# A transformer kernel on one core: maxima bank by bank, and its loads cut into pieces and put in another order

## The chip, the cores and the metric

The kernel runs on 1 core of one Trainium2 chip. The metric is the device time of one execution in microseconds. Before the change three runs took 503.15, 505.49 and 505.87 us: the median is 505.49 us.

## The reference

Batch 2, 12 heads, 448 tokens, head size 64. First an attention that mixes its heads before and after the softmax, then two blocks of multi-layer mixing. q, k, v are 32 bit; the weights of the two later blocks come as 64-bit floats and are turned into 32-bit pairs (high and low) on the chip.

```python
scores = scale * np.matmul(q, k.transpose(0, 1, 3, 2))
scores = np.einsum('bhij,hg->bgij', scores, w_pre)
scores = scores - np.max(scores, axis=-1, keepdims=True)
attn = np.exp(scores)
attn = attn / (np.sum(attn, axis=-1, keepdims=True) + 1e-09)
attn = np.einsum('bhij,hg->bgij', attn, w_post)
attn_out = np.matmul(attn, v)
...
u = x + (np.maximum(x.T @ w_tok1, 0) @ w_tok2).T
x = u + np.maximum(u @ w_ch1, 0) @ w_ch2
h = gelu(x @ w_in); u, v = halves(h); v_n = layer norm of v
out = x + (u * (w_sg @ v_n + b_sg)) @ w_out
```

## The kernel before, in words

**Chunks.** The rows of each batch are cut into four chunks (`CH`, line 45: 120, 120, 120 and 88 rows). For one chunk and one pair of heads `qk` (line 318) multiplies q by k: eight matmuls into a PSUM tile of two banks, which ScalarE or VectorE then copies into the score tile S of the chunk. Chunks 0 and 1 are computed ahead of the loop (lines 520 to 525); `COPIES` (line 518) says which engine copies which pair of heads, and for the last pair of each of these two chunks the copy is split: one engine takes the first bank, the other the second. Later chunks' `qk` are spread over the steps (lines 526 to 531).

**Steps.** A step works on 20 rows of a chunk with all 12 heads (the last step of a batch on 8 rows). There are 46 steps, 23 for each batch. For a step, `b_dma` (line 352) moves scores from S into two P tiles by DMA (210 KB each), heads and rows now on the partitions. `b_pre` mixes heads by matmuls into a PSUM pair, two banks for two groups of rows; `b_max` (line 369) takes the negative maximum of each row, both banks by one VectorE reduction; `b_exp` is one ScalarE instruction per bank with the maximum as bias and the sum as second output; `b_norm` on GpSimd inverts the sums and scales the mixing weights; `b_post` (line 399) mixes heads again with 64 small matmuls; `b_turn` copies the result into AT. Once a chunk is complete, `av` (line 425) multiplies AT by v and copies the two banks of its PSUM pair, the first by ScalarE, the second by VectorE (line 457).

**Order.** The order on each engine is written out by hand in the loop of line 566, which runs from -5 to 45. In turn i stand `b_pre`, `b_max` and `b_exp` of step i + 2 (`LP`), `b_norm` of step i + 1, `b_post` and `b_turn` of step i, an `av` where one is due, then on SP's queue `b_dma` of step i + 5 (`LD`), and after it the loads that the list at line 537 gives for that turn. There are eight P tiles, so the `b_dma` of step i + 5 waits until the pre of step i + 1 has read its tiles. `b_dma` of step 0 stands ahead of the loop (line 565), its second half on ScalarE's queue; all other loads but one are on SP's queue.

**Loads.** `load_q` brings half of the q of a chunk (192 KB), `load_v` a third of v (448 KB), `load_k` one pair of heads of k or two (`KG`, line 309: 224 KB, once 448 KB). The first four weight pieces (448 to 512 KB, "early", line 82) are loaded in attention, one at a time: the first from the list at turn 6, each following one when the piece ahead of it has been converted.

**The pump.** `conv_steps` (line 160) is a generator that converts the weight pieces: absolute value on ScalarE, a clamp (for early pieces on GpSimd), three bit operations on VectorE, a cast on ScalarE, a subtraction on GpSimd, about one instruction for each turn of the generator. In attention the loop turns it once a step from step 8 on (`pump(1)`, line 596). An early piece takes eight turns in all, the fourth one seven.

Of the kernel before, what the change touches and what calls it, by code (L numbers as in the profile page):

```python
# [8 lines left out]
F32 = mybir.dt.float32  # L9
F32R = mybir.dt.float32r  # L10
U32 = mybir.dt.uint32
# [4 lines left out]
ALU = mybir.AluOpType  # L16
AX = mybir.AxisListType
PSUM = bass.MemoryType.PSUM

LD, LP = 5, 2  # L20
NP_BUFS = 2 * (LD - LP + 1)
# [9 lines left out]
def tile_kernel(ctx, tc, q, k, v, w_pre, w_post, w_tok1, w_tok2, w_ch1, w_ch2,  # L31
                w_u, w_v, g_ln, w_sg, b_sg, w_out, out):
    nc = tc.nc
    B, D, H, S = 2, 64, 12, 448
    P = 128
    NP = H // 2
# [43 lines left out]
    wstate = {"dma": 0, "conv": 0, "room": 0, "used": 0, "bar": 0, "raw": {}, "abs": {}, "open": False}  # L80

    def early(i):

        return i <= p_t2[-1]

    def w_dma():
        i = wstate["dma"]
        if i >= len(pieces) or not (early(i) or wstate["open"]):
            return
        wstate["dma"] += 1  # L90
        src, pr, a, n = pieces[i][:4]
        wide = 1 if src.dtype == F32 else 2
        if early(i):
            raw = ap_.tile([P, 2 * EC], U32, tag="eraw", name=f"raw{i}")
        else:
            raw = wpool.tile([P, 2 * WC], U32, tag="raw", name=f"raw{i}", bufs=RB)
        r = raw[:pr, :wide * a * n].rearrange("p (a n) -> p a n", a=a)
        nc.sync.dma_start(out=r, in_=src.bitcast(U32))
        wstate["raw"][i] = r

# [59 lines left out]
    def conv_steps():  # L160
        for i in range(len(pieces)):
            while i not in wstate["raw"]:
                yield
            for _ in w_conv(i):
                yield
            wstate["conv"] = i + 1
            w_dma()
            yield
            if early(i + 1):
                yield  # L170

    def pump(n):

# [112 lines left out]
    ap_ = actx.enter_context(tc.tile_pool(name="attn", bufs=1))  # L286
    psM = actx.enter_context(tc.tile_pool(name="psM", bufs=2, space=PSUM))
    psB = actx.enter_context(tc.tile_pool(name="psB", bufs=2, space=PSUM))
# [9 lines left out]
    QG = 3  # L298
    NQ = NP // QG

    def load_v(b, g):
        t = vn[b, g] = ap_.tile([P, 14 * D], F32, tag=f"vn{g}", name=f"vn{b}_{g}")
        nc.sync.dma_start(out=t, in_=v[b, :, g])

    def load_q(b, c, g, eng=nc.sync):
        t = qn[b, c, g] = qp.tile([P, QG, P], F32, tag=f"qn{g}", name=f"qn{b}_{c}_{g}", bufs=2)
        eng.dma_start(out=t, in_=q[b, :, c, g * QG:(g + 1) * QG])

    KG = [(0, 1), (1, 1), (2, 2), (4, 1), (5, 1)]

    def load_k(b, g):
        i, n = KG[g]
# [30 lines left out]
    NB = len(steps)  # L343
# [5 lines left out]

    ring = [ap_.tile([P, S], F32, name=f"P{n}") for n in range(NP_BUFS)]  # L350

    def b_dma(i, engines=(nc.sync, nc.sync)):

        b, c, p, ne = steps[i]
        nb = CH[c][1] // (2 * IB)
        for r in range(2):
            j = 64 * r + p
            src = SS[b, c][j:j + (IB - 1) * nb + 1:nb] if ne == 2 else SS[b, c][64 * r + IB * nb:64 * r + IB * nb + HB]
            engines[r].dma_start(out=ring[(2 * i + r) % NP_BUFS][PAD:PAD + ne * HW], in_=src)

    def b_pre(i):
        ne = steps[i][3]
# [6 lines left out]
    def b_max(i):  # L369
        ne = steps[i][3]  # L370
        st[i]["nm"] = ap_.tile([P, 2], F32, tag="nm", name=f"nm{i}", bufs=3)
        nc.vector.tensor_reduce(out=st[i]["nm"][:, :ne], in_=st[i]["pre"][:, :ne, :S], axis=AX.X, op=ALU.max, negate=True)  # L372

    def b_exp(i):
        ne = steps[i][3]
# [110 lines left out]
    def add(step, fn, *a):  # L486
        extra.setdefault(step, []).append((fn, a))
# [27 lines left out]
    nc.gpsimd.memset(mone, -1.0)  # L515
    turn_over(8)

    COPIES = ((nc.scalar.copy, nc.vector.tensor_copy), (nc.vector.tensor_copy, nc.scalar.copy))
    scores = {}
    for x in range(NCH):  # L520
        if x < 2:
            at = [-LD - 1 + x] * NP
            for i in range(NP):
                n = x * NP + i
                add(at[i], qk, x, i, (psM, psB)[n % 2], COPIES[n % 2][:1 + (n == NP - 1)])
        else:
            f0, f1 = first[chunks[x - 1]] - LD, first[chunks[x]] - LD
            room = list(range(f0, f1))
            at = [room[i * len(room) // NP] for i in range(NP)]
            for i in range(NP):  # L530
                scores.setdefault(at[i], []).append((x, i))
        if x == 0:
            add(at[-1], scale_pre)
    for fn, a in extra.pop(-LD - 1):
        fn(*a)
    loads = {}
    for at, fn, *a in [(-2, load_q, 0, 2, 0), (-1, load_q, 0, 2, 1), (1, load_v, 0, 1), (3, load_v, 0, 2),
                       (4, load_q, 0, 3, 0), (6, load_q, 0, 3, 1), (6, load_q, 1, 0, 0), (6, w_dma),
                       (9, load_k, 1, 0), (9, load_k, 1, 1), (9, load_q, 1, 0, 1),
                       (12, load_k, 1, 2), (12, load_k, 1, 3), (14, load_k, 1, 4),  # L540
                       (15, load_const_late), (15, load_q, 1, 1, 0), (15, load_q, 1, 1, 1),
                       (18, load_q, 1, 2, 0), (20, load_q, 1, 2, 1), (23, load_q, 1, 3, 0), (26, load_q, 1, 3, 1),
                       (26, load_v, 1, 0), (27, load_v, 1, 1), (29, load_v, 1, 2)]:
        loads.setdefault(at, []).append((fn, a))

    X, RX = {}, {}
# [15 lines left out]
        if i + LD > NB and turns:  # L562
            turn(pair(f"xps0_{len(turns)}")[:, 0], *turns.pop(0))

    b_dma(0, (nc.sync, nc.scalar))
    for i in range(-LD, NB):
        for fn, a in extra.get(i, []):
            fn(*a)
# [18 lines left out]
            b_turn(i, nc.vector.tensor_copy if ahead else nc.scalar.copy)  # L587
            next_av(i)
        next_turn(i)
        if 0 < i + LD < NB:  # L590
            b_dma(i + LD)
        for fn, a in loads.get(i, []):
            fn(*a)
        if 0 < i + LD - NB <= RB:
            w_dma()
        if i >= 8:
            pump(1)
        if i + LD == NB:
            qctx.close()
# [412 lines left out]
```

## Time and profile before

| | |
|---|---|
| median of 3 runs | 505.49 us (503.15 to 505.87) |
| the profiled execution | 505.07 us, its span 503.3 us |
| TensorE busy | 482.0 us (96% of the span) |
| VectorE, ScalarE, GpSimd busy | 341.7, 235.5, 209.5 us |
| bytes moved | 63.84 MB, mean 127 GB/s |

Times in rows are microseconds from the start of the span. PE is TensorE, PEld its weight loads, DVE VectorE, ACT ScalarE, POOL GpSimd, SP SyncE; a q behind the name is the engine's queue of instructions that do no work of their own, such as issuing a DMA. L372 is line 372 of the kernel. A tile goes by its name without its number, as `nm<-pre`: written from read. "issue" as a releaser means that the engine waited for nothing that the profile shows. A matmul with 32-bit operands shows as two records, so four matmuls of `b_pre` are eight.

### The profile page before, as it was taken

The numbers are of one execution on the slowest core, as the hardware profiler recorded it, in microseconds if no ns is written. First come the engines' busy times: TensorE is split into PE (matmuls) and PEld (weight loads), VectorE is DVE, ScalarE is ACT, GpSimd is POOL, SyncE is SP. The second block draws the span as 40 slices with busy tenths as digits, with TensorE's granted clock in tenths as the row PEclk, the third lists the DMA queues.
The fourth block names the chain that finished last, engine by engine and source line by source line (L and its number), as shares of the span: only waits on it lengthen the run. The fifth ranks groups of instructions, "written<-read, shape, count | busy, mean of one in ns | idle before, by whom it ended". The sixth has DMA issues, their size and how long they took to land.

```text
span 503.3 us, 14004 instructions
## 1 busy us (share of the span) xinstructions
PE 482.0 (96%) x6010; PEld 407.4 (81%) x6010; DVE 341.7 (68%) x453; ACT 235.5 (47%) x456; POOL 209.5 (42%) x292
## 2 busy tenths in 40 slices
PE   9698799999998889999999999999999999999997
PEld 5256576766776679999999999999999998888996
DVE  2566466667758646735577587788987874898882
ACT  3566567567765535533334344342433344454320
POOL 2244446446565401481213223544454533258500
PEclk9999999999999999999999999999999999999999
DMA  6577665557643601301325333443433324003222
GB/s 215 172 229 238 190 186 169 165 179 222 210 130 118 199 3 64 125 1 63 105 73 179 104 126 113 136 150 127 130 121 104 106 73 137 21 0 118 84 78 110
DMA packets 26018, 63.84 MB, mean 127 GB/s; under 512 B 2868, under 2 KB 19300, under 8 KB 25956
## 3 DMA queue, kind: packets, MB, share of 16 engines
q1 hardware_dynamic: 25682, 62.53, 38.9%
q8 instruction: 47, 0.77, 0.6%
q10 hardware_dynamic: 274, 0.41, 0.3%
q14 instruction: 15, 0.12, 0.1%
HBM read 40.83 MB, written 2.75 MB: 87 GB/s over the span
## 4 chain that ended last, share of the span: by engine, by line
PE 87%; ACT 3%; DVE 3%; issue 3%; DMA 2%; POOL 1%; SPq 0%; POOLq 0%; ACTq 0%
PE qk L327 7%; PE post L414 7%; PE av L444 6%; PE c2ps L622 6%; PE c1ps L622 6%; PE c2ps L624 6%; PE c1ps L624 6%; PE c1ps L623 6%; PE c2ps L623 6%; PE pre L367 5%; PE ups L623 2%; PE ups L622 2%; PE ups L624 2%; PE vps L623 2%; PE vps L622 2%
## 5 line engine op out<-in xcount | busy, mean ns | idle before, releaser
L155 POOL TENSOR_TENSOR wl<-cv,wh 128x768 fp32r<-128x768 f32 x28 | 52.6, 1880 | 135.2 <-ACT wh L152 103.8
L380 ACT ACTIVATE E<-pre,nm 128x448 f32<-128x448 f32 x90 | 56.4, 632 | 37.2 <-DVE nm L372 33.4
L414 PEld LDWEIGHTS post<-wt,E 60*64 60x64 f32 x2880 | 52.8, 136 | 24.3 <-issue 13.8
L372 DVE TENSOR_REDUCE nm<-pre 128x2 f32<-128x896 f32 (+1 forms) x46 | 49.2, 1069 | 23.6 <-PE pre L367 19.3
L414 PE MATMUL post<-wt,E 60*64 60x60 f32 (+1 forms) x2880 | 54.0, 219 | 3.9 <-issue 1.6
L134 DVE SCALAR_TENSOR_TENSOR cv<-raw,cv 128x768 uint32<-128x768 uint32 (+2 forms) x44 | 53.1, 1207 | 1.1
L327 PE MATMUL qk<-kn,qn 64*64 64x448 f32 x384 | 48.0, 561 | 4.8 <-ACT S L332 2.5
L622 PE MATMUL c1ps<-uh,wh 128*128 128x448 f32 x144 | 52.3, 363 | 0.0
L622 PE MATMUL c2ps<-r1h,wh 128*128 128x448 f32 x144 | 52.3, 363 | 0.0
L624 PE MATMUL c1ps<-uh,wl 128*128 128x448 f32 x144 | 52.2, 362 | 0.0
L624 PE MATMUL c2ps<-r1h,wl 128*128 128x448 f32 x144 | 52.2, 362 | 0.0
L367 PE MATMUL pre<-P,wp 64*64 64x448 f32 (+1 forms) x360 | 49.1, 540 | 3.0 <-DMA P<-S 2.0
L623 PE MATMUL c1ps<-ul,wh 128*128 128x448 f32 x144 | 51.8, 360 | 0.0
L623 PE MATMUL c2ps<-r1l,wh 128*128 128x448 f32 x144 | 51.8, 360 | 0.0
L422 DVE COPY AT<-post 128x840 f32<-128x840 f32 (+1 forms) x44 | 46.1, 1048 | 3.2 <-PE post L414 3.0
L112 ACT ACTIVATE cv<-raw 128x768 f32<-128x768 f32 (+2 forms) x44 | 36.2, 822 | 25.0 <-POOL wl L155 17.8
L387 POOL TENSOR_SCALAR rc<-sm 128x2 f32<-128x2 f32 (+1 forms) x46 | 10.5, 229 | 82.0 <-ACT E L380 81.4
L332 ACT COPY S<-qk 128x896 f32<-128x896 f32 (+1 forms) x43 | 38.5, 899 | 12.8 <-PE qk L327 12.3
L136 DVE SCALAR_TENSOR_TENSOR cv<-raw,cv 128x768 uint32<-128x768 uint32 (+2 forms) x44 | 40.3, 916 | 1.0
L152 ACT CAST wh<-cv 128x768 fp32r<-128x768 f32 x28 | 23.4, 835 | 34.6 <-DVE cv L136 33.6
L645 DVE SCALAR_TENSOR_TENSOR r1l<-c1ps,r1h 128x448 fp32r<-128x448 f32 x24 | 15.0, 624 | 30.6 <-ACT r1h L643 30.6
L444 PE MATMUL av<-AT,vn 128*64 128x120 f32 (+1 forms) x576 | 32.6, 268 | 3.1 <-issue 2.3
(146 smaller groups left out, 1026.7 us busy)
## 6 DMA issues: line engine op xcount, KB each, us to landing
raw<-in_w_ch_dram SPq DMA_DIRECT2D x24, 768.0 KB
P<-S SPq DMA_DIRECT2D x87, 210.0 KB
raw<-in_w_v_dram SPq DMA_DIRECT2D x6, 512.0 KB
raw<-in_w_u_dram SPq DMA_DIRECT2D x4, 768.0 KB
raw<-in_w_out_dram SPq DMA_DIRECT2D x6, 512.0 KB
qn<-in_q_dram SPq DMA_DIRECT2D x15, 192.0 KB
vn<-in_v_dram SPq DMA_DIRECT2D x6, 448.0 KB
out_dram<-xT SPq DMA_DIRECT2D x12, 224.0 KB
```

The lines of the kernel that those rows point to most:

```text
L134: nc.vector.scalar_tensor_tensor(fi, lo, 29, fi, op0=ALU.logical_shift_right, op1=ALU.bitwise_or)
L155: nc.gpsimd.tensor_tensor(dst[1], f, f32(dst[0]), op=ALU.subtract)
L327: nc.tensor.matmul(ps[cols, j, :S], lhsT=qn[b, c, i // QG][rows, i % QG, cols], rhs=KX[b, i][rows], start=True, stop=True)
L367: nc.tensor.matmul(ps[cols, e, :S], lhsT=wp[rs], rhs=ring[(2 * i + r) % NP_BUFS][rs], start=True, stop=True)
L372: nc.vector.tensor_reduce(out=st[i]["nm"][:, :ne], in_=st[i]["pre"][:, :ne, :S], axis=AX.X, op=ALU.max, negate=True)
L380: nc.scalar.activation(t, st[i]["pre"][:, e, :S], AF.Exp, bias=st[i]["nm"][:, e:e + 1], scale=1.0, accum_out=sm[:, e:e + 1])
L414: nc.tensor.matmul(ps[cols, r, o:o + w.stop - w.start], lhsT=E[rs, t * 64:(t + 1) * 64], rhs=wt[rs, w], start=True, stop=True)
L422: copy(dst.rearrange("p g (a i) -> p a g i", i=HB), src.rearrange("p a (g i) -> p a g i", i=HB))
L444: nc.tensor.matmul(into(hp, x, j), lhsT=vn[b, hp // 2][:, ((hp % 2 * 2 + j) * NH + s) * D:][:, :D], rhs=at[:, s * H + 2 * hp + j, :cols], ...
L622: nc.tensor.matmul(ps, lhsT=lh, rhs=rh, start=(start and i == 0), stop=False)
L623: nc.tensor.matmul(ps, lhsT=lh, rhs=rl, start=False, stop=False)
L624: nc.tensor.matmul(ps, lhsT=ll, rhs=rh, start=False, stop=(stop and i == n - 1))
```

## The change

- `b_max` writes two reductions in place of one, one for each bank, each into its own column of nm.
- `COPIES` gives each of the first twelve score tiles to one engine whole, VectorE first, and the last pair of each of the two chunks is no longer split.
- `b_dma` of step 0 moves into the loop (turn -5) and both its halves are on SP's queue.
- `KG` has six single pairs of heads. `load_v` can take half of its columns. Early weight pieces are loaded in two halves of 64 partitions, with one turn of the pump between them; such a piece takes nine turns.
- The list of loads is another one: q of the third rows goes from turns -2 and -1 to -4 and -3, and of the others most turns issue one piece.
- The loop turns the pump from step 9 on instead of step 8.

```diff
-    def w_dma():
+    def w_dma(half=None):
...
+        if half == 1:
+            r, src = wstate["half"]
+            nc.sync.dma_start(out=r[64:], in_=src[64:])
+            wstate["raw"][i] = r
+            wstate["dma"] += 1
+            return
+        wstate["dma"] += half is None
...
+        if half == 0:
+            wstate["half"] = r, src.bitcast(U32)
+            nc.sync.dma_start(out=r[:64], in_=wstate["half"][1][:64])
+            return
...
-            w_dma()
+            if early(i + 1):
+                w_dma(0)
+                yield
+                w_dma(1)
+                yield
+            else:
+                w_dma()
             yield
-            if early(i + 1):
-                yield
...
-    def load_v(b, g):
-        t = vn[b, g] = ap_.tile([P, 14 * D], F32, tag=f"vn{g}", name=f"vn{b}_{g}")
-        nc.sync.dma_start(out=t, in_=v[b, :, g])
+    def load_v(b, g, h=None):
+        if not h:
+            vn[b, g] = ap_.tile([P, 14 * D], F32, tag=f"vn{g}", name=f"vn{b}_{g}")
+        o = slice(0, 14 * D) if h is None else slice(7 * D * h, 7 * D * (h + 1))
+        nc.sync.dma_start(out=vn[b, g][:, o], in_=v[b, :, g, o])
...
-    KG = [(0, 1), (1, 1), (2, 2), (4, 1), (5, 1)]
+    KG = [(i, 1) for i in range(NP)]
...
-        nc.vector.tensor_reduce(out=st[i]["nm"][:, :ne], in_=st[i]["pre"][:, :ne, :S], axis=AX.X, op=ALU.max, negate=True)
+        for e in range(ne):
+            nc.vector.tensor_reduce(out=st[i]["nm"][:, e:e + 1], in_=st[i]["pre"][:, e, :S], axis=AX.X, op=ALU.max,
+                                    negate=True)
...
-    COPIES = ((nc.scalar.copy, nc.vector.tensor_copy), (nc.vector.tensor_copy, nc.scalar.copy))
+    COPIES = (nc.vector.tensor_copy,), (nc.scalar.copy,)
...
-                add(at[i], qk, x, i, (psM, psB)[n % 2], COPIES[n % 2][:1 + (n == NP - 1)])
+                add(at[i], qk, x, i, (psM, psB)[n % 2], COPIES[n % 2])
...
-    for at, fn, *a in [(-2, load_q, 0, 2, 0), (-1, load_q, 0, 2, 1), (1, load_v, 0, 1), (3, load_v, 0, 2),
-                       (4, load_q, 0, 3, 0), (6, load_q, 0, 3, 1), (6, load_q, 1, 0, 0), (6, w_dma),
-                       (9, load_k, 1, 0), (9, load_k, 1, 1), (9, load_q, 1, 0, 1),
...
+    for at, fn, *a in [(-4, load_q, 0, 2, 0), (-3, load_q, 0, 2, 1),
+                       (0, load_v, 0, 1, 0), (1, load_v, 0, 1, 1), (2, load_v, 0, 2, 0), (3, load_v, 0, 2, 1),
+                       (4, load_q, 0, 3, 0), (5, load_q, 1, 0, 0), (6, w_dma, 0), (7, w_dma, 1), (8, load_q, 0, 3, 1),
+                       (9, load_k, 1, 0), (10, load_k, 1, 1), (11, load_k, 1, 2), (12, load_k, 1, 3),
+                       (12, load_q, 1, 0, 1), (13, load_k, 1, 4), (14, load_k, 1, 5), (15, load_q, 1, 1, 0),
...
-    b_dma(0, (nc.sync, nc.scalar))
...
-        if 0 < i + LD < NB:
+        if i + LD < NB:
             b_dma(i + LD)
...
-        if i >= 8:
+        if i >= 9:
             pump(1)
```

## Rows read from the trace of the kernel before

**Rows 1.** Busy time by stretch: stretch, length, engines (instructions), granted clock, DMA share, GB/s

```profile
36.00:60.00 24.00, 20.33 (x561) 15.00 (x554) 12.92 (x15) 14.71 (x34) 12.10 (x28) 1.00 0.77 227
...
160.00:166.00 6.00, 5.35 (x216) 4.18 (x210) 5.67 (x7) 3.57 (x11) 3.75 (x10) 1.00 0.41 91
...
174.00:190.00 16.00, 13.83 (x325) 11.97 (x317) 7.24 (x14) 5.37 (x14) 1.53 (x5) 0.89 0.01 3
190.00:300.00 110.00, 110.00 (x585) 102.79 (x585) 71.01 (x106) 47.19 (x77) 39.17 (x26) 1.00 0.29 96
```

**Rows 2.** Waits of TensorE, whole span: total us, times, longest

```profile
PE qk L327 <- ACT S L332: 2.5, 3, 1.0
PE av L444 <- issue: 2.3, 1, 2.3
PE qk L327 <- DMA qn<-in_q_dram: 2.0, 1, 2.0
PE pre L367 <- DMA P<-S: 2.0, 3, 1.0
PE post L414 <- issue: 1.6, 3, 1.0
PE post L414 <- POOL wt L393: 1.1, 2, 0.5
...
PE pre L367 <- ACT E L380: 0.6, 1, 0.6
```

**Rows 3.** Timeline, 6 to 26 us: start, length, instruction, idle before it and releaser

```profile
7.58 1.09 DVE L332 COPY S<-qk 128x896 f32<-128x896 f32 x1 [6.59 <-PE qk L327]
...
8.33 0.91 ACT L332 COPY S<-qk 128x896 f32<-128x896 f32 x1 [0.83 <-PE qk L327]
...
10.58 0.62 DVE L332 COPY S<-qk 128x448 f32<-128x448 f32 x1 [0.41 <-PE qk L327]
...
11.24 0.53 ACT L332 COPY S<-qk 128x448 f32<-128x448 f32 x1 [0.50 <-DVE S L332]
...
11.80 1.40 ACTq L359 DMA_DIRECT2D P<-S  x1
...
14.21 1.73 PE L327 MATMUL qk<-kn,qn 64*64 64x448 f32 x16 [0.69 <-ACT S L332]
...
20.46 1.39 SPq L307 DMA_DIRECT2D qn<-in_q_dram  x1
...
25.56 0.98 PE L327 MATMUL qk<-kn,qn 64*64 64x448 f32 x8 [2.00 <-DMA qn<-in_q_dram]
```

**Rows 4.** Busy time by stretch, as in rows 1: plain loads, then mostly P tiles

```profile
6.00:8.00 2.00, 2.00 (x20) 0.68 (x16) 0.42 (x1) 0.91 (x1) 0.00 (x0) 1.00 1.05 379
20.00:22.00 2.00, 2.00 (x10) 0.60 (x12) 1.03 (x1) 0.59 (x2) 1.14 (x3) 1.00 0.60 197
```

**Rows 5.** Waits of SP's queue: what the issue of P tiles waits for

```profile
SPq L359 <- PE post L414: 48.5, 41, 4.9
```

**Rows 6.** The chain that ended last, two steps in a row: start, length, piece

```profile
25.56 0.98 PE qk L327 x8
...
28.20 0.78 PE qk L327 x8
```

**Rows 7.** Groups of instructions up to 190 us: count, busy us, mean ns, idle before

```profile
L372 DVE TENSOR_REDUCE nm<-pre 128x2 f32<-128x896 f32 x44 | 47.9, 1090 | 23.6 <-PE pre L367 19.3 <-issue 3.4 <-ACT E L380 0.8
...
L372 DVE TENSOR_REDUCE nm<-pre 128x1 f32<-128x448 f32 x2 | 1.2, 616 | 0.0
```

**Rows 8.** Waits of all engines, one line: total us, times, longest

```profile
DVE xT L461 <- ACT xT L461: 26.8, 12, 4.5
```

**Rows 9.** Timeline, three instructions between 100 and 155 us

```profile
102.91 0.61 ACT L152 CAST shared<-cv 128x512 fp32r<-128x512 f32 x1
...
150.85 0.62 DVE L134 SCALAR_TENSOR_TENSOR cv<-raw,cv 128x448 uint32<-128x448 uint32 x1
...
153.95 0.98 PE L367 MATMUL pre<-P,wp 64*64 64x448 f32 x8 [0.63 <-ACT E L380]
```

More of the change, by code (lines that the diff above doesn't have):

```diff
@@ L89, in w_dma @@
             return
-        wstate["dma"] += 1
+        if half == 1:
[5 more added lines that the diff above has]
+        wstate["dma"] += half is None
         src, pr, a, n = pieces[i][:4]
@@ L350, in tile_kernel, with b_dma @@
     ring = [ap_.tile([P, S], F32, name=f"P{n}") for n in range(NP_BUFS)]
-    def b_dma(i, engines=(nc.sync, nc.sync)):
+    def b_dma(i):
         b, c, p, ne = steps[i]
@@ L358, in b_dma @@
             src = SS[b, c][j:j + (IB - 1) * nb + 1:nb] if ne == 2 else SS[b, c][64 * r + IB * nb:64 * r + IB * nb + HB]
-            engines[r].dma_start(out=ring[(2 * i + r) % NP_BUFS][PAD:PAD + ne * HW], in_=src)
+            nc.sync.dma_start(out=ring[(2 * i + r) % NP_BUFS][PAD:PAD + ne * HW], in_=src)
     def b_pre(i):
@@ L536, in tile_kernel @@
     loads = {}
-    for at, fn, *a in [(-2, load_q, 0, 2, 0), (-1, load_q, 0, 2, 1), (1, load_v, 0, 1), (3, load_v, 0, 2),
-                       (4, load_q, 0, 3, 0), (6, load_q, 0, 3, 1), (6, load_q, 1, 0, 0), (6, w_dma),
-                       (9, load_k, 1, 0), (9, load_k, 1, 1), (9, load_q, 1, 0, 1),
[L540 to L543, printed above, removed]
+    for at, fn, *a in [(-4, load_q, 0, 2, 0), (-3, load_q, 0, 2, 1),
[3 more added lines that the diff above has]
+                       (12, load_q, 1, 0, 1), (13, load_k, 1, 4), (14, load_k, 1, 5), (15, load_q, 1, 1, 0),
+                       (16, load_const_late), (17, load_q, 1, 1, 1), (21, load_q, 1, 2, 0), (23, load_q, 1, 2, 1),
+                       (24, load_v, 1, 0, 0), (25, load_v, 1, 0, 1), (26, load_q, 1, 3, 0), (27, load_v, 1, 1, 0),
+                       (28, load_v, 1, 1, 1), (29, load_q, 1, 3, 1), (30, load_v, 1, 2, 0), (31, load_v, 1, 2, 1)]:
         loads.setdefault(at, []).append((fn, a))
```

## The prediction

> **What bounds the kernel now.** I read the stage table first. From 190 us on TensorE hardly pauses (110.00 of 110.00 us up to 300 us) [rows 1]; the change moves only the start of what runs there, so that part slides. What can be won lies in attention, ahead of 190 us, and there it is TensorE's idle time, since its work stays the same. The list of TensorE's waits names it [rows 2]: 2.0 us for a q tile, 2.0 us for P tiles, 2.5 us for score copies on ScalarE, 3.9 us (2.3 + 1.6, four waits) in which nothing that the profile shows was missing ("issue"), and 0.6 and 1.1 us for the exp and the weights of the last steps. The timeline shows where these stand: the q tile is awaited at 25.56 us, one copy at 14.21 us [rows 3]. VectorE, ScalarE and the DMA queue matter only where they end one of these waits.
>
> **The start (steps -5 to 1).** Before, q of the third rows is issued at 20.46 us, behind the P tiles of steps 0 to 3, and TensorE stands 2.00 us until 25.56 us [rows 3]. After, it is issued behind the P tiles of step 1, four P issues earlier, and should be there when the first post ends. It now passes ahead of the P tiles of step 2: 192 KB at the 379 GB/s of plain loads [rows 4] are 0.5 us, and the first post stands behind the pre of step 2. The second half of step 0's P moves from ScalarE's queue to SP's. That frees 1.40 us of ScalarE, the reason of the 0.69 us wait at 14.21 us [rows 3]; in exchange SP issues one more transfer first. The last copy of the first chunk goes from two halves in a row (until 11.77 us) to one ScalarE copy of 0.91 us, which would end at 10.58 + 0.91 = 11.49 us, 0.28 us sooner [rows 3]. Ends: at least 2.0 - 0.5 = 1.5 us, and where P is late 0.5 us less again, 1.0; at most 2.0 + 0.28 + 0.69 and the half of the P waits that stands ahead of the first pre, 4.0. Behind the q wait P tiles are what is late next, so I take little beyond it: **-2.3 us**.
>
> **One load a step.** Loads of 448 to 512 KB become halves, the k pair two singles: 5 more issues for v, 4 for early weights, 2 for k. Eleven issues of up to 1.39 us [rows 3] are 15 us of SP's queue, covered by the 48.5 us in which SP waits for post to free P tiles [rows 5]; without that cover P would be issued late. Per step the queue moves two P tiles, 430 KB at 197 GB/s (almost only P moved then) = 2.2 us, and a piece of 224 KB at 379 GB/s = 0.6 us [rows 4], less where they overlap (P alone fills only 0.60 of the engines). A step without av takes 28.20 - 25.56 = 2.64 us [rows 6]. So the first steps are near balance, and better spread than before, where 640 KB of k and q and a 512 KB weight piece came in bursts. The "issue" waits lie where DMA was busiest, 0.77 in 36 to 60 us [rows 1]. If bursts delayed the instruction stream, all 3.9 us could go; if plain load did, none, and steadier load could add 1.0. No row tells the two apart; I take 40%: **-1.6 us**.
>
> The Trainium skill, in "DMA: Bandwidth & Descriptors", section "Rules for kernel authors", asks for transfers of 1 MiB or more and advises against splitting one by partition halves, since both halves use the same engines. The row speaks against a loss here: 192 and 224 KB loads together moved 379 GB/s [rows 4]. By the rule the smaller pieces would gain nothing, and the sum would lose the 1.6 us: 502.2 us.
>
> **Two maxima a step.** One reduction of 1090 ns becomes two of 616 ns [rows 7]: 142 ns more VectorE time in each of 44 steps, 6.2 us in all. The gain would be that the exp of bank 0 starts after 616 instead of 1090 ns, 0.47 us sooner. The traces speak against that start. Where two engines read the two banks of one PSUM pair, the second waits for the first: the second half of the split score copy began 0.04 us after VectorE's half, having idled 0.50 us [rows 3], and twelve VectorE copies of av's second bank waited 26.8 us in all for ScalarE's copy of the first [rows 8]. Their destination isn't the cause: copies into one S from two PSUM tiles overlap (7.58 + 1.09 against 8.33 us) [rows 3]. The second maximum stands ahead of the first exp, so I expect that exp to wait for both. Then the exps come 0.14 us later. In most steps two steps of lead hide it; on the path I count four places (the two later score-copy waits, two steps of the tail), 0.6 us, and 0.4 us for steps in which a conversion on VectorE stands beside the longer maxima. Ends: four times 0.47 us won, or 6.2 us lost. I take **+1.0 us**.
>
> The Trainium skill, "Advanced Engine Details and Errata", section "Bank Collisions", has ScalarE and VectorE reading PSUM at full rate together when they use different banks. By that the exp would start early and the sum be 2.5 us lower; the waits of av's copies say that this program doesn't let it come to that.
>
> **Conversions moved.** The pump starts at step 9 instead of 8, and each of the first three weight pieces takes nine turns instead of eight. So the fourth piece is converted in steps 36 to 42 instead of 32 to 38, and all others slip by one to three steps. The cast of 0.61 us in ScalarE's queue ahead of a score copy at 102.91 us [rows 9] goes elsewhere; of the two later copy waits (2.5 - 0.69 = 1.8 us) I take that much, **-0.6 us**, ends 0 and -1.8. At 150.85 us a conversion of 0.62 us stands on VectorE ahead of a maximum whose exp holds up pre by 0.63 us at 153.95 us [rows 9], and behind it a post by 0.5 us [rows 2]; with that conversion gone both go, 1.1 us, of which 0.1 for the longer maximum stays: **-1.0 us**. The same conversions then land in 160 to 166 us, where VectorE has 5.67 of 6.00 us filled [rows 1]; the other end is that two of 0.62 us are paid there, +1.2 us.
>
> **Sum.** -2.3 (start) - 1.6 (loads) + 1.0 (maxima) - 0.6 - 1.0 (conversions) = -4.5 us. The profiled execution took 505.07 us (span 503.3 us), so **500.6 us**. The median of the runs, 505.49, is 0.4 us above it, well within their spread.
>
> **Rivals.**
> A. *The early exp works.* Against it stand [rows 3, 8]. It would take 0.47 us from the four places instead of adding: 500.6 - 2.5 = 498.1 us.
> B. *The wait is only handed on.* The instruction stream is late under even load too, and P tiles, now behind q and with a piece between each pair, take over the q wait. For it: per step 2.8 us of transfers against 2.64 us of work, if nothing overlapped. Against: before, the same bytes went through in these steps without a P wait after 20 us. Only 1.0 us of the start and 0.6 and 1.0 of the conversions stay, less 1.0 for the maxima: 503.5 us.
> C. *Slower: VectorE becomes the bound of the steps.* Place: maximum, turn copy and conversion of each step, in order on one queue, with 0.14 us more and the fourth piece's conversions in the tail. If all 6.2 us and 1.2 us land on the path while the gains of start and loads (3.9) stand: 505.07 + 7.4 - 3.9 = 508.6 us. It decides as soon as VectorE has no idle time left in the steps around a conversion, as in 160 to 166 us; against it, 36 to 60 us has it at 12.92 of 24 us [rows 1].
>
> **Numbers.** My forecast has 0.46 (its own range 498 to 503), A 0.17, B 0.23, C 0.14. What this kernel's measurement can tell from no change is about 0.5%, 2.5 us around 505.5. Under 503.0: 0.38 of the forecast, all of A, a fifth of B (0.05), together 0.60. Over 508.0: most of C, 0.12. The rest, 0.28, is no change. Left over in all cases: the stretch from 174 to 190 us, where the granted clock averages 0.89 after idle turns [rows 1], may gain or lose the 1.8 us that this is. The range goes from just under A to between B and C: 496.8 to 506.2.
>
> **What would show it.** Right: the qk of the third rows no longer waits, at 22.5 to 23.5 us; no wait of the second chunk's qk for ScalarE at 14 us; "issue" waits between 36 and 60 us down to about half; the first exp of a step starting right after the second maximum, and VectorE 6 us busier. Wrong: exps that start between the two maxima (A), pre waiting for P between 24 and 45 us (B), post waiting for weights or for turn copies in steps with a conversion (C).

## The result and the profile after

The changed kernel takes 510.64 us (median of 17 runs, 507.02 to 513.78), the kernel before 505.87 us (17 runs on the same chip): the ratio is 1.0109 [1.0082, 1.0135]. The ratio is taken over fast runs alone (none over 1.5% above the fastest of its kernel), the medians over all, and their ratio is 1.0094. The change is slower by about 5 us, where 500.6 us was forecast.

The profiled execution of the changed kernel took 507.89 us, its span is 506.1 us; before, 505.07 and 503.3. From the first matmul of the first token layer (`t1ps`, at 189.36 us before and 191.62 after) to the end it is 313.9 before and 314.5 after: 2.26 of the 2.8 us are lost ahead of it, in attention. This execution is the third fastest of the 17, so it shows a part of the 5 us only.

Where in attention, the copy of a step's result into AT tells: it exists in both kernels and comes once a step. Steps 1, 15 and 30 of the kernel before (start, length, instruction):

```profile
28.46 1.06 DVE L422 COPY AT<-post 128x840 f32<-128x840 f32 x1
...
78.07 1.06 DVE L422 COPY AT<-post 128x840 f32<-128x840 f32 x1
...
132.24 1.06 DVE L422 COPY AT<-post 128x840 f32<-128x840 f32 x1
```

The same steps of the changed kernel:

```profile
26.80 1.06 DVE L440 COPY AT<-post 128x840 f32<-128x840 f32 x1
...
75.18 1.06 DVE L440 COPY AT<-post 128x840 f32<-128x840 f32 x1
...
134.50 1.06 DVE L440 COPY AT<-post 128x840 f32<-128x840 f32 x1
```

The change is 1.66 us ahead in step 1 and 2.89 in step 15, and 2.26 us behind in step 30. The start brought 1.66 us by step 1, where 2.3 was forecast; 5.15 us were lost between 75 and 135 us.

The table by stretch, of the kernel after; columns as in [rows 1], whose stretches stand here in the first and the last three rows:

```profile
36.00:60.00 24.00, 21.41 (x582) 15.05 (x576) 13.83 (x20) 14.45 (x34) 11.20 (x25) 1.00 0.73 217
60.00:100.00 40.00, 37.25 (x1010) 27.49 (x1007) 24.62 (x38) 25.68 (x58) 20.35 (x47) 1.00 0.57 170
100.00:120.00 20.00, 17.42 (x524) 12.37 (x517) 13.88 (x22) 13.39 (x33) 9.99 (x24) 1.00 0.65 189
120.00:150.00 30.00, 29.04 (x831) 21.45 (x832) 20.69 (x33) 20.38 (x47) 15.15 (x35) 1.00 0.59 174
160.00:166.00 6.00, 5.73 (x175) 4.26 (x170) 4.46 (x9) 1.71 (x5) 3.65 (x9) 1.00 0.24 52
174.00:190.00 16.00, 12.34 (x290) 10.47 (x292) 6.85 (x12) 7.13 (x18) 2.68 (x7) 0.89 0.04 12
190.00:300.00 110.00, 110.00 (x620) 102.72 (x617) 71.25 (x107) 46.47 (x79) 38.35 (x26) 1.00 0.29 90
```

and the three stretches from 60 to 150 us of the kernel before:

```profile
60.00:100.00 40.00, 39.21 (x1056) 28.59 (x1049) 26.41 (x33) 26.37 (x60) 20.14 (x47) 1.00 0.57 171
100.00:120.00 20.00, 18.16 (x544) 13.33 (x542) 12.84 (x16) 14.38 (x36) 11.34 (x24) 1.00 0.63 189
120.00:150.00 30.00, 29.91 (x864) 22.41 (x860) 21.31 (x26) 21.20 (x49) 16.82 (x39) 1.00 0.58 182
```

From 36 to 60 us TensorE is idle 2.6 us, where it was 3.7 [rows 1]: better. From 60 to 150 us it is idle 2.75 + 2.58 + 0.96 = 6.3 us, where it was 0.79 + 1.84 + 0.09 = 2.7. VectorE is not full there (24.62 of 40), and the DMA share is the same within 0.02, so neither a full VectorE nor more transfers took the time. TensorE's waits in the whole span, after (total us, times, longest), against [rows 2]:

```profile
PE post L432 <- issue: 2.7, 3, 1.1
PE av L462 <- issue: 2.5, 2, 1.6
PE pre L383 <- DMA P<-S: 2.1, 5, 0.6
PE av L471 <- issue: 1.4, 2, 1.2
PE post L432 <- POOL wt L411: 1.1, 2, 0.5
...
PE qk L343 <- DMA qn<-in_q_dram: 0.7, 1, 0.7
...
PE av L462 <- ACT S L348: 0.6, 1, 0.6
...
PE qk L343 <- ACT S L348: 0.5, 1, 0.5
```

The waits for score copies fell from 2.5 to 1.1 us, that for q from 2.0 to 0.7, and the 0.6 us for the exp at the tail is gone. But "issue", the wait for nothing that the profile shows, rose from 4.2 to 6.6 us; by stretch, from 3.7 to 1.9 ahead of 60 us and from 0.6 to 4.8 between 60 and 150.

What such a wait is can be seen at 84 us in the kernel after:

```profile
82.18 0.88 PE L432 MATMUL post<-wt,E 60*64 60x60 f32 x42
84.14 0.45 PE L432 MATMUL post<-wt,E 60*64 60x60 f32 x16 [1.09 <-issue]
...
84.42 0.27 PE L432 MATMUL post<-wt,E 60*64 60x30 f32 x6
```

A `post` is 64 matmuls on operands that are all there when it begins. It stops after 42 of them, for 1.09 us. No data was missing, so the instructions were. The profile's page counts their transfers on a queue of their own, 47 in both kernels, 0.77 MB in all, 16 KB each:

```profile
q8 instruction: 47, 0.77, 0.7%
```

The profile names no releaser, but the packets of this queue stand in the trace with their times. Around this stop one of them ran from 81.52 to 82.70 us and the next came at 87.15. This is what the view shows from 81.4 to 82.8 us and from 86.9 to 88.2; between 82.9 and 83.9 it has none:

```profile
q8 instruction: 1, 0.02, 5.3%
...
q8 instruction: 1, 0.02, 4.5%
```

TensorE went on at 84.14, 1.45 us after the first had ended, and so it is at every stop. The 20 traces of this case hold 133 issue waits of TensorE, and each of them ends 1.1 to 1.7 us after the end of one of these transfers (median 1.44), though in attention the transfers come only about every 5 us. The place in the program is fixed too: counted over TensorE's records, matmuls and weight loads together, all 133 waits end at the same record of every 256, to within one; 47 transfers for some 12,110 records are one for 258. So TensorE waited there for a block of its own instructions that came late. Below, "issue" stands for this wait.

The transfers didn't take longer, they began later. Between 60 and 150 us one takes 1.08 us on average before and 1.14 after. But from the moment that TensorE is 320 records ahead of the place where it needs the block, the transfer begins 2.3 us later on average before (at most 3.4), and 3.2 after (at most 5.6). In the 20 traces this delay and the sum of issue waits in that stretch correlate with 0.93. What delays the beginning, the traces don't show.

### The profile page after: what moved, and what is told of

It reads as the page before. It is cut to its first block, busy times and chain, and to the rows that moved or that the text cites. A ratio compares the mean times of both kernels' runs of the same rounds, so it can differ in the third digit from the quotient of the medians.

```text
span 506.1 us, 14067 instructions
## 1 busy us (share of the span) xinstructions
PE 484.6 (96%) x6010; PEld 408.4 (81%) x6010; DVE 345.7 (68%) x497; ACT 234.9 (46%) x455; POOL 209.2 (41%) x292
## 3 DMA queue, kind: packets, MB, share of 16 engines
HBM read 40.83 MB, written 2.75 MB: 86 GB/s over the span
## 4 chain that ended last, share of the span: by engine, by line
PE 83%; ACT 5%; DVE 4%; DMA 3%; issue 3%; POOL 1%; POOLq 0%; SPq 0%; ACTq 0%
PE qk L343 6%; PE av L462 6%; PE c2ps L640 6%; PE c1ps L640 6%; PE c2ps L642 6%; PE c1ps L642 6%; PE c2ps L641 6%; PE c1ps L641 6%; PE post L432 6%; PE pre L383 5%; ACT E L398 3%; DVE nm L389 2%; PE ups L641 2%; PE ups L640 2%; PE ups L642 2%
## 5 line engine op out<-in xcount | busy, mean ns | idle before, releaser
L389 DVE TENSOR_REDUCE nm<-pre 128x1 f32<-128x448 f32 x90 | 51.9, 618 | 21.7 <-PE pre L383 17.9
L432 PE MATMUL post<-wt,E 60*64 60x60 f32 (+1 forms) x2880 | 55.9, 220 | 5.2 <-issue 2.7
L383 PE MATMUL pre<-P,wp 64*64 64x448 f32 (+1 forms) x360 | 50.9, 541 | 2.4 <-DMA P<-S 2.1
L348 ACT COPY S<-qk 128x896 f32<-128x896 f32 x42 | 38.0, 906 | 11.7 <-PE qk L343 11.1
```

What stands on the lines that cost most here:

```text
L383: nc.tensor.matmul(ps[cols, e, :S], lhsT=wp[rs], rhs=ring[(2 * i + r) % NP_BUFS][rs], start=True, stop=True)
L389: nc.vector.tensor_reduce(out=st[i]["nm"][:, e:e + 1], in_=st[i]["pre"][:, e, :S], axis=AX.X, op=ALU.max, negate=True)
L432: nc.tensor.matmul(ps[cols, r, o:o + w.stop - w.start], lhsT=E[rs, t * 64:(t + 1) * 64], rhs=wt[rs, w], start=True, stop=True)
```

## The experiments

Each kernel below the first two rows was timed in five rounds beside the kernel before on the same chip, on four chips in all. "Issue" is the sum of TensorE's issue waits in the one profiled execution of each, up to 60 us and from 60 to 150 us. Old turns are eight turns a piece from step 8, new turns nine from step 9.

| kernel | against before | issue, to 60 / 60 to 150 us | span, us |
|---|---|---|---|
| before | 1 | 3.7 / 0.6 | 503.3 |
| after | 1.0109 [1.0082, 1.0135] | 1.9 / 4.8 | 506.1 |
| before + two maxima (x1) | 1.0019 [0.9979, 1.0059] | 3.3 / 1.0 | 504.3 |
| before + new start (x2) | 0.9970 [0.9934, 1.0006] | 2.9 / 1.1 | 499.7 |
| before + new loads (x3) | 1.0002 [0.9964, 1.0039] | 1.4 / 1.6 | 500.8 |
| before + weights part (x4) | 1.0053 [1.0016, 1.0090] | 4.1 / 1.9 | 505.0 |
| after, weights part as before (y1) | 1.0006 [0.9970, 1.0042] | 0.3 / 0.8 | 500.4 |
| before + new turns (y2) | 1.0051 [1.0016, 1.0086] | 0 / 6.2 | 503.6 |
| after, halves by columns (y3) | 1.0069 [1.0029, 1.0108] | 4.0 / 4.6 | 508.1 |
| after, one maximum (y4) | 1.0102 [1.0066, 1.0139] | not compared: granted clock 0.987 | |
| before + step 9 alone (z1) | 1.0013 [0.9973, 1.0052] | 3.9 / 2.6 | 504.6 |
| before + nine turns alone (z2) | 1.0018 [0.9979, 1.0057] | 2.1 / 2.9 | 504.1 |
| after, old turns (z3) | 1.0026 [0.9991, 1.0061] | 0.8 / 2.0 | 506.9 |
| y2, transfers earlier (z4) | 1.0013 [0.9974, 1.0052] | 0 / 1.9 | 500.9 |
| after, transfers earlier (v1) | 1.0136 [1.0088, 1.0184] | 0.9 / 8.1 | 509.8 |
| after, without transfers (v2) | 1.0038 [1.0005, 1.0071] | 2.2 / 2.9 | 505.1 |
| after, step 8 (v3) | 1.0075 [1.0035, 1.0115] | 2.5 / 1.1 | 502.7 |
| before + start + loads + early transfers (v4) | 1.0043 [1.0009, 1.0078] | 3.3 / 2.4 | 505.1 |
| old turns without transfers (u1) | 1.0010 [0.9974, 1.0046] | 2.6 / 2.0 | 504.8 |
| after without conversions (u2) | 1.0055 [1.0016, 1.0093] | 2.7 / 4.9 | 505.3 |

TensorE's granted clock enters both the spans and the ratios. In most executions it is at its lower level (1.2 instead of 2.4 GHz) for some microseconds, in the two kernels' profiles at 176 to 179 us (after) and 174 to 178 (before). The profiled x2, x3, y1, y2 and z1 have no such stretch ahead of 490 us (mean clock 0.999 to 1.000), x4 and z3 the most of those compared (0.991 and 0.993). The record has the mean clock of each timed run too: with each kernel's own level taken out, a run is 4.7 us shorter for 0.01 more clock. "At equal clock" below means that a difference was corrected by this line, with a 95% interval of about 1.3 us on either side; whether a kernel's clock is luck or its own doing, the record doesn't tell.

### Each part alone

x1, the two maxima:

```diff
-        nc.vector.tensor_reduce(out=st[i]["nm"][:, :ne], in_=st[i]["pre"][:, :ne, :S], axis=AX.X, op=ALU.max, negate=True)
+        for e in range(ne):
+            nc.vector.tensor_reduce(out=st[i]["nm"][:, e:e + 1], in_=st[i]["pre"][:, e, :S], axis=AX.X, op=ALU.max,
+                                    negate=True)
```

> The kernel before with two maxima a step and nothing else of the change. Theory F (TensorE waits for its own instructions: the loads now keep the DMA engines busy in every step and the fetches of TensorE's code start late): the maxima do little, 0 to +1 us. Rival V (VectorE: 6 us more of it, exps later): +3 to +5 us, with post or qk waiting for exp, weights or copies.

x2, the start: whole copies, `b_dma` of step 0 in the loop on SP's queue, q of the third rows at -4 and -3:

```diff
...
-        for at, fn, *a in [(-2, load_q, 0, 2, 0), (-1, load_q, 0, 2, 1),
+        for at, fn, *a in [(-4, load_q, 0, 2, 0), (-3, load_q, 0, 2, 1),
...
-    b_dma(0, (nc.sync, nc.scalar))
...
```

> The kernel before with the start of the change alone: q of the third rows at turns -4 and -3, whole score copies, both P halves of step 0 on SP's queue. All theories: -1.5 to -2.5 us, the wait for q gone, since the trace after had that lead from step 1 on. If it is 0, the lead is given back later whatever the loads are.

x3, the list of loads with k and v in pieces; q of the third rows and the weights as before:

```diff
...
-    KG = [(0, 1), (1, 1), (2, 2), (4, 1), (5, 1)]
+    KG = [(i, 1) for i in range(NP)]
...
```

> The kernel before with the loads of k, v and q as changed (k one by one, v in halves, the new turns) but q of the third rows, the weight pieces and the pump as before. Theory F: +3 to +6 us, with more issue waits of TensorE (4.2 us before, 6.6 after) between 75 and 130 us. Rival V: 0.

x4, the weights part: early pieces in halves, nine turns, pump from step 9:

```diff
...
+            if early(i + 1):
+                w_dma(0)
+                yield
+                w_dma(1)
+                yield
...
-        if i >= 8:
+        if i >= 9:
```

> The kernel before with the early weight pieces in halves and the pump from step 9 on, nothing else. Theory F: 0 to +1 us. Third theory P (conversions land in other steps and stand in front of maxima and copies there): +2 to +4 us, with waits of post and qk for VectorE, ScalarE or GpSimd in the last ten steps.

Measured in us of 505.5: maxima +1.0 (-1.1 to +3.0), start -1.5 (-3.3 to +0.3), loads +0.1 (-1.8 to +2.0), weights +2.7 (0.8 to 4.5). Only the weights part is slower for certain.

### Each part taken out of the change

y1, the change with the weights part as before (whole pieces, old turns):

```diff
...
-                       (4, load_q, 0, 3, 0), (5, load_q, 1, 0, 0), (6, w_dma, 0), (7, w_dma, 1), (8, load_q, 0, 3, 1),
+                       (4, load_q, 0, 3, 0), (5, load_q, 1, 0, 0), (6, w_dma), (8, load_q, 0, 3, 1),
...
-        if i >= 9:
+        if i >= 8:
```

> The changed kernel with the early weight pieces whole again and the pump from step 8, as before. Theory W (the weights' part costs most, and more where its halves meet the halves of v): back to 504 to 507 us, issue waits near 4 us. Rival V (two maxima cost in company of the other parts): still 509 us or more.

y2, the kernel before with the new turns alone, its pieces whole:

```diff
             w_dma()
             yield
             if early(i + 1):
                 yield
+                yield
...
-        if i >= 8:
+        if i >= 9:
```

> The kernel before with whole weight pieces, but nine turns of the pump for each and the pump from step 9: the conversions stand where the change puts them, the transfers stay whole. Theory H (it is the halves): the time of before, within 1 us. Theory P (it is where the conversions land): +2 to +3 us, as with the weights' part.

y3, the change with its halves cut by columns, over all 128 partitions:

```diff
...
-            nc.sync.dma_start(out=r[64:], in_=src[64:])
+            nc.sync.dma_start(out=half_of(r, 1), in_=half_of(src, 1))
...
```

> The changed kernel with each early weight piece cut along its columns, so that both halves write all 128 partitions instead of 64 each. If a half over 64 partitions keeps the engines longer, 506 to 508 us and fewer issue waits; if only the number and place of the transfers count, 510 us as the change.

y4, the change with one maximum for both banks:

```diff
-        for e in range(ne):
-            nc.vector.tensor_reduce(out=st[i]["nm"][:, e:e + 1], in_=st[i]["pre"][:, e, :S], axis=AX.X, op=ALU.max,
-                                    negate=True)
+        nc.vector.tensor_reduce(out=st[i]["nm"][:, :ne], in_=st[i]["pre"][:, :ne, :S], axis=AX.X, op=ALU.max, negate=True)
```

> The changed kernel with one maximum over both banks again. Theory W: 509.5 to 510.5 us (the maxima alone were worth 0.2%). Rival V: 506 to 508 us, exps 0.07 us sooner in every step.

y1 takes the loss away (1.0006; at equal clock 1.3 of 4.8 us stay, 0 to 2.6); in its trace TensorE's issue waits from 60 to 150 us are two of 0.4 us:

```profile
PE av L448 <- issue: 0.4, 1, 0.4
PE post L418 <- issue: 0.4, 1, 0.4
```

One maximum changes nothing (y4). The new turns alone cost as much as the whole weights part (y2 against x4), so no halves are needed for a loss. Partition halves against column halves (1.0109, 1.0069) can't be told apart. The weights part measures more in the change (1.0109 against 1.0006, +1.0%) than in the kernel before (+0.5%), but the intervals overlap.

### The turns taken apart

z1, the kernel before with the pump from step 9; z2, the same with nine turns a piece and step 8; z3, the change with its halves, but old turns:

```diff
-        if i >= 8:
+        if i >= 9:
```

> The kernel before with one edit: the pump starts in step 9 instead of 8, eight turns a piece. Every conversion and each following weight transfer moves by one step. Theory 'the shift costs as it grows': the loss of +2.6 us that nine turns and step 9 made together (shifts of 1, 2, 3 and 4 steps for the four pieces) falls to about a third, +0.9 us, 506.5 with 505.6 for the kernel before. Rival 'it's the places of pieces 2 and 3': nothing is lost in steps 19 to 28, since these pieces move by one step only: within 0.5 us of before. Rival 'the one step is enough': +2 us or more, 507.7.

```diff
             if early(i + 1):
                 yield
+                yield
```

> The kernel before with one edit: nine turns for each of the first three weight pieces, the pump from step 8 as before. Pieces 1 to 4 move by 0, 1, 2 and 3 steps. Theory 'the shift costs as it grows': about two thirds of +2.6 us, 507.3. Rival 'places of pieces 2 and 3': most of it, +2 us, 507.7. Rival 'the one step at the start is what costs': no loss, 505.6.

```diff
                 w_dma(1)
-                yield
             else:
...
-        if i >= 9:
+        if i >= 8:
```

> The changed kernel with its halves of weight pieces kept, but eight turns a piece and the pump from step 8, so conversions stand in the steps where the kernel before has them. Theory 'the moved turns are the loss': as the changed kernel with the whole weights part undone, 506 to 507. Rival 'the halves cost, and the moved turns only when alone': 509.5 to 510.6, as the changed kernel.

z4, y2 with the next piece's transfer issued right behind the last read of the piece ahead, two turns earlier; v1, the same in the change, for both halves:

```diff
             nc.vector.scalar_tensor_tensor(fi, hi, 0xC0000000, fi, op0=ALU.bitwise_and, op1=ALU.bitwise_or)
+            if early(i + 1):
+                w_dma()
...
```

> The kernel before with nine turns a piece and the pump from step 9, but the next piece's transfer is issued as soon as the piece ahead has been read for the last time, two turns earlier: steps 13, 22 and 31 instead of 15, 24 and 33 (14, 22 and 30 in the kernel before). The conversions stand where the changed kernel has them, the transfers nearly where the kernel before has them. Theory 'the weight transfers' place makes the instruction fetches late': no loss, 505.6 to 506.2, issue waits of TensorE at most 4.5 us in all. Rival 'the conversions' place on ScalarE, VectorE and GpSimd is the loss': 508.3 as with nine turns alone, issue waits or not.

```diff
             nc.vector.scalar_tensor_tensor(fi, hi, 0xC0000000, fi, op0=ALU.bitwise_and, op1=ALU.bitwise_or)
+            if early(i + 1):
+                w_dma(0)
...
             nc.scalar.copy(dst[0], f)
+            if early(i + 1):
+                w_dma(1)
...
```

> The changed kernel whole, but the halves of the next weight piece are issued as soon as the piece ahead has been read for the last time: in turns 13 and 14, 22 and 23, 31 and 32 in place of 15 and 16, 24 and 25, 33 and 34. No conversion moves. Theory 'the place of the weight transfers makes the instruction fetches late': most of the loss goes, 506 to 507.5, and TensorE's issue waits are 2 to 4 us in the trace. Rival 'the conversions' places on the engines are the loss': 510 to 511, as the changed kernel.

v3, the change with the pump from step 8:

```diff
-        if i >= 9:
+        if i >= 8:
```

> The changed kernel with one number back: the pump from step 8. Pieces 2 to 4 still come 1 to 3 steps later than in the kernel before, and the halves stay. Theory 'each step of shift costs its part': about half of the loss stays, 508 to 509. Rival 'one start of the pump collides': none stays, 506 to 507. Rival 'nine turns are what costs': all stays, 510 to 511.

With the halves kept and the turns put back (z3), most of the loss goes by the ratios: 1.0109 to 1.0026, a difference of 0.83% (0.39 to 1.27, the two intervals taken as independent). At equal clock z3 is still 2.2 us slower than before (0.9 to 3.5) and the change 4.8 by its medians, so by either count half of the loss or more is the turns. Either half of the shift alone gives 1.0013 and 1.0018 on the kernel before, with 1 inside the intervals, and v3 lies between z3 and the change. That looks as if the loss grew with the shift, but it isn't shown: the runs of z1 had a mean clock of 0.9967 and those of the kernel before beside them 0.9940. At equal clock z1 is 3.2 us slower, z2 1.7 and both together (y2) 2.5, not to be told apart. z4 looked as if earlier transfers were the cure (issue 1.9 us, 1.0013); v1 refutes that in the change itself: 1.0136 (six runs; 5.0 us slower at equal clock), and the largest sum of issue waits of all between 60 and 150 us:

```profile
PE post L434 <- issue: 6.4, 5, 2.6
PE av L464 <- issue: 1.1, 2, 0.6
...
PE av L473 <- issue: 0.6, 1, 0.6
```

### Transfers or conversions

v2, the change without the transfers of pieces 2 to 4; u1, the same in z3; u2, the change with these transfers but without the conversions:

```diff
-            nc.sync.dma_start(out=r[64:], in_=src[64:])
+            if not i:
+                nc.sync.dma_start(out=r[64:], in_=src[64:])
...
-        if early(i):
+        if early(i) and i:
+            raw = wstate["eraw"]
+        elif early(i):
...
```

> The changed kernel without the transfers of the second, third and fourth weight piece; their conversions stand where they were and read the first piece again (left out: 1.4 MB of loads, so the two token layers mix with wrong weights). Theory 'transfers': 506 or less, as the changed kernel with the old weights part, and issue waits under 3 us. Rival 'conversions': 510 to 511, with issue waits of 6 us or more all the same.

> The changed kernel with the conversions back in their old turns (eight a piece, from step 8) and without the transfers of the second to fourth weight piece, whose conversions read the first piece again (left out: 1.4 MB of loads). Its pair is the changed kernel without these transfers (1.0038); the two differ by the places of the conversions alone. Theory 'conversions and transfers each cost their own': the places cost 0.8% with transfers (1.0109 against 1.0026), so also without: 0.995 to 0.996, 502.5 to 503. Rival 'only both together cost': the places alone cost next to nothing: 1.002 to 1.004, 506 to 507.

```diff
         src, pr, a, n, scale, dst = pieces[i]
+        if early(i) and i:
+            for _ in range(6):
+                yield
+            pieces[i][5] = tok_dst(0, pr, a, n)()
+            return
```

> The changed kernel with all its transfers in place, but the 21 conversion instructions of the second to fourth weight piece are left out (the blocks behind use the first piece's weights). Theory 'the conversions' places on ScalarE, VectorE and GpSimd make the loss': nothing of it stays and the work itself is saved, 503 to 506. Rival 'the transfers at these steps make the fetches late': 509 to 511, with issue waits of 6 us or more.

Without the transfers 0.71% of the time goes (0.29 to 1.13, worked out as above), without the conversions 0.54% (0.07 to 1.01). By these ratios neither rival is right alone: the 21 conversions at their new places without transfers leave 1.0038, the transfers without them 1.0055. The second figure leans on the clock: the runs of u2 had a mean clock of 0.9967, those of the kernel before beside them 0.9943. At equal clock u2 is 4.5 us slower (3.1 to 5.9), about as much as the change by its medians (4.8), and v2 2.2 us (0.9 to 3.5). So about half the loss goes with the transfers; that the conversions have a part of their own isn't shown. With old turns the transfers cost no more than these runs can tell (z3 1.0026, u1 1.0010). The traces lean to the transfers: without conversions TensorE's issue waits between 60 and 150 us are as long as in the change, 4.9 us,

```profile
PE post L437 <- issue: 3.1, 4, 1.2
PE av L467 <- issue: 0.9, 1, 0.9
PE av L476 <- issue: 0.9, 1, 0.9
```

without transfers 2.9 us:

```profile
PE post L436 <- issue: 1.5, 3, 1.0
PE av L475 <- issue: 1.4, 1, 1.4
```

### A version from the parts that lost nothing

v4: start and loads on the kernel before, one maximum, whole pieces, old turns, the transfers two turns earlier as in z4:

```diff
...
-    COPIES = ((nc.scalar.copy, nc.vector.tensor_copy), (nc.vector.tensor_copy, nc.scalar.copy))
+    COPIES = (nc.vector.tensor_copy,), (nc.scalar.copy,)
...
-    KG = [(0, 1), (1, 1), (2, 2), (4, 1), (5, 1)]
+    KG = [(i, 1) for i in range(NP)]
...
             nc.vector.scalar_tensor_tensor(fi, hi, 0xC0000000, fi, op0=ALU.bitwise_and, op1=ALU.bitwise_or)
+            if early(i + 1):
+                w_dma()
...
```

> Put together from what lost nothing: the kernel before with the changed start (q of the third rows earlier, whole score copies) and the smaller loads in their new order, one maximum, whole weight pieces with eight turns from step 8, and each next piece issued two turns earlier, when the piece ahead has been read. If start (0.997) and loads (1.000) add up and the earlier transfers help the fetches: 503 to 505. If a gain at the start is lost again in the steps, as in the changed kernel with the old weights part: 505.5 to 507.

It beats nothing: 1.0043, against 0.9970 and 1.0002 for start and loads alone. That it is slower than before, with transfers earlier and conversions where they were, speaks with v1 against the cure. No kernel tried is faster than the one before for certain; the new start alone comes nearest, 0.9970 [0.9934, 1.0006].

## Why the prediction was wrong

**The step that failed is "Conversions moved", forecast at -1.6 us.** It looked for the waits that the moved instructions leave and arrive at, and it was right on most of them: the later waits for score copies fell by 0.7 us (1.8 to 1.1), where a fall of 0.6 was taken, and the 0.63 us wait for the exp at the tail went. Of the 1.1 us of `post` behind `wt`, of which 0.5 was to go, nothing went. What was won at the tail was nearly lost again there: by the copies into AT the change makes up 1.0 us from step 35 to 37 and falls back 1.6 us by step 41, and over the steps 35 to 45 0.2 us are left. There the conversions did arrive where the other end of the forecast had put them, with VectorE full from 162 to 166 us (4.46 of 6.00 from 160 to 166, against 5.67 in [rows 1]):

```profile
162.00:166.00 4.00, 3.73 (x132) 2.46 (x120) 4.00 (x9) 1.34 (x4) 1.92 (x5) 1.00 0.22 36
```

What the step left out is what the move does away from these places, at no price in the sum: the same edit moves three weight transfers of 448 to 512 KB by one, two and three steps, and issue waits came up between 60 and 150 us, where there had been 0.6 us. Measured, the step costs +2.6 us alone (y2), and in the change +4.2 us (1.0109 less 1.0026 of 505.5; 2.6 at equal clock).

**The start, -2.3 us: right in kind.** q is issued at 14.96 us, no longer awaited, and the first exp follows:

```profile
14.96 1.02 SPq L323 DMA_DIRECT2D qn<-in_q_dram  x1
...
16.96 1.15 DVE L389 TENSOR_REDUCE nm<-pre 128x1 f32<-128x448 f32 x2 [2.30 <-PE pre L383]
...
18.22 0.64 ACT L398 ACTIVATE E<-pre,nm 128x448 f32<-128x448 f32 x1 [2.98 <-DVE nm L389]
...
23.02 0.98 PE L343 MATMUL qk<-kn,qn 64*64 64x448 f32 x6
```

The third rows' qk begins within 22.5 to 23.5 us, as forecast, where it stood at 25.56 [rows 3]. The time by itself, -1.5 us, has -2.3 in its interval, and 0.

**Loads, -1.6 us: the size was off.** The place was right and the gain is seen there: issue waits between 36 and 60 us fell from 3.7 to 1.9 us, "about half". But it brought no time by itself (x3: +0.1 us, -1.8 to +2.0).

**Maxima, +1.0 us: right**, as far as it can be measured (+1.0 in x1, none in y4), and in the order: the first exp starts at 18.22 us, after both maxima (16.96, two within 1.15 us). By "Bank Collisions" in the Trainium skill's "Advanced Engine Details and Errata" ScalarE and VectorE can read two different banks of PSUM at full rate together. This trace doesn't test that: the exp's wait is put down to nm, one tile into which both maxima write, and whether nm or the PSUM pair made it wait no run tells. The price in VectorE time was taken too high: a pair of maxima takes 1.15 us together and not twice 0.62, so 44 of them cost 2.8 us more than single ones of 1.09, not 6.2. VectorE's busy time is 345.7 us for 341.7.

**The rivals.** A fell with that exp. B did not come: waits for P tiles are 2.1 us where they were 2.0 [rows 2], and the wait for q that is left (0.7 us, fourth rows) is new and small. C gave the nearest number (508.6), but by the wrong cause where the time was lost: VectorE has idle time in every stretch from 60 to 150 us, and is full only from 162 to 166, where 1.6 us went and half of it came back later. What came, late instructions outside the stretch where they were late before, was no rival. The prediction had seen issue waits, had said that no row tells their cause, and had allowed 1.0 us more of them for the loads alone; for the moved weight transfers it allowed none.

**What is shown and what stays open.** Shown by the timed runs: half of the loss or more comes with the moved turns (z3, y2), it needs no halves (y2) and no second maximum (y4), and about half of it goes when pieces 2 to 4 are not transferred (v2). Shown by the traces: the issue waits are waits for blocks of TensorE's instructions whose transfers begin late. That these waits are the loss is likely, not proved. Over the 19 profiled executions that have a span in the table, span and total issue wait correlate with 0.79, and a straight line through them rises 0.96 us for each us waited; each is one execution, and the granted clock has its part in it. In the change itself the clock is 1.00 in each stretch from 36 to 150 us, so there the clock isn't the cause. Open: why these turns make the instructions late. It isn't the step of the transfers alone: z3 issues its halves in turns 14 and 15, 22 and 23, 30 and 31, v1 in 13 and 14, 22 and 23, 31 and 32, and they lie 1.1% apart (0.6% at equal clock). What separates them is where the conversions stand; but without the conversions and with the transfers where the change has them (u2) the time at equal clock is that of the change. No kernel without conversions and with the transfers in their old turns was tried. Nor was one with other sizes or places of TensorE's instruction transfers, which would test directly what the waits cost.

## What to carry to other kernels

A yield more in a generator that issues transfers moves transfers as well as arithmetic: price all that it issues, and the instruction stream beside it. Where an engine stops in the middle of matmuls whose operands are there, treat the schedule as tuned against its instruction transfers: forecast moves of other traffic with a range on both sides, and look for such waits in every stretch, not only where they stand now. To tell such a wait from others, lay the times of the instruction queue's packets beside it. A gain at the start of a pipeline counts only once it is still there at the end of it, so compare one instruction per step across both traces. Where differences of some tenths of a per cent decide, compare the granted clocks of the runs as well as their times.

## What the runs showed of the hardware that was not expected

- TensorE's stops in mid-`post` reached 2.6 us for one (v1), and there were up to 9.1 us of issue waits in one execution (y3; 9.3 in y4), with the same 47 instruction transfers in each kernel. Each of the 133 stops ended 1.1 to 1.7 us after such a transfer had ended, at the same record of every 256.
- Such a stop can cost more than its length. In seven traces (x4, y3, y4, z2, v3, v4, u1) the granted clock falls to its lower level within 1.1 us of the end of an issue wait of 1.7 to 2.2 us. In v3 the wait of 1.8 us ends at 36.5 us:

```profile
37.00:40.00 3.00, 3.00 (x50) 2.04 (x49) 1.06 (x1) 0.45 (x2) 1.54 (x4) 0.50 0.76 233
```

  Longer ones can go without it: 2.3 us before, 2.4 in z1 and 2.6 in v1 were not followed by a lower clock.
- A weight half of 256 KB can take 7 us to land, and the conversion that waits for it holds up the score copy behind it in ScalarE's queue. In z3, whose second half is issued in turn 7 and read from step 8 on, the chain of waits shows it (start, length, piece):

```profile
47.31 7.04 DMA raw<-in_w_tok_dram
54.36 0.02 issue
54.38 0.05 ACT cv L122
54.43 0.52 issue
54.94 0.90 ACT S L347
55.84 0.04 issue
55.88 3.87 PE av L461 x36
```

  The score copy came late, and `av` waited 3.9 us for it; its 36 matmuls then took 3.87 us at the lower clock (0.50 from 56 to 60 us), where they take 2.07 at 158 us in the change.

```profile
PE av L461 <- ACT S L347: 3.9, 1, 3.9
```

  Neither the change nor v3, which issues and reads that half in the same turns as z3, has such a wait, so it is one execution's and says nothing for step 9.
- Two maxima of one bank each take 1.15 us together where one over both takes 1.09; in [rows 7] one of a single bank takes 0.62.
